# An adaLN block's modulation: rows of w_mod as TensorE weights for all columns, in place of summed and turned rows

## Chip, core and metric

The kernel runs on one core of one Trainium2 chip. Its time is the device time of one execution in microseconds (us); lower is better. The core has five engines that run their own instruction streams: TensorE (PE: matmuls, with weight loads shown apart as PEld), VectorE (DVE), ScalarE (ACT), GpSimd (POOL) and SyncE (SP, which issues nearly all DMAs).

## The reference, cut to what matters

`x` is 2048 tokens of 576, in float32. A condition vector `c` of 576 gives six vectors of 576: shift, scale and gate of an attention block (a) and of a feed-forward block (b).

```python
mod = (_silu(c) @ w_mod).reshape(c.shape[0], 6, 1, -1)
sa, ca, ga, sb, cb, gb = (mod[:, 0], ..., mod[:, 5])
h = _layernorm(x, axis=-1) * (1 + ca) + sa
x = x + ga * _A_ref(h, A_wqkv, A_wo)      # linear attention, 32 heads of 18
h = _layernorm(x, axis=-1) * (1 + cb) + sb
x = x + gb * _B_ref(h, B_w1, B_w2)        # feed-forward, 576 -> 4608 -> 576, silu
```

Nothing of the attention can be computed before `sa` and `ca` are there: the first 1152 columns of `silu(c) @ w_mod`. The change is in how these two vectors are made.

## The kernel before, in words

**Layout.** The tokens are 16 tiles of 128, in four blocks of 512. The 576 features are five chunks (`START`): four of 128 and a tail of 64. For a matmul the normalised `x` is turned so that features lie on partitions; there shift and scale of a chunk are two columns, `cols["a"][:, k, 0:2]`, each with one number per partition. `modulate` (L210) applies them, and `split_h` (L218) cuts the float32 result into a rounded part (a cast on ACT, L220) and a remainder (a subtraction on DVE, L136). Weights are cut in the same way by `w_hi` (ACT, L359) and `w_lo` (L364, L366; on DVE or POOL). Each product takes three passes: high by high, low by high, high by low.

**The first two vectors.** `silu(c)` lies in `sc`, chunk k in column k. w_mod's first 1152 columns come as five chunks of rows: `mods[0]` to `mods[3]` (128 rows each, seen as two times 576 columns) and `tmod` (the last 64 rows, with shift's columns on partitions 0 to 63 and scale's on 64 to 127). SP loads columns 0 to 255 of the four chunks first (`load_mod0(0, HEAD * P)`), then two chunks of the k weights, then the other columns.

For chunks 0 and 1 of the columns (`HEAD = 2`, 256 columns) DVE scales `mods[0]` by `sc`'s column in place (L413) and adds the three other chunks times theirs (L415). `mod_cols` (L417) then takes the sums and `tmod` as weights, 128 columns at a time, against a column of ones (`sel` for `tmod`): the result is a column per chunk in PSUM, `colp[k]`. `add_cols` (L427, one DVE instruction, L429) copies the columns of some chunks to `cols["a"]` and adds 1 to the scales.

For chunks 2 to 4 (320 columns) DVE sums in the same way (one L413 and three L415 of 640 elements). Then `mod_rows` (L431) uses `ones` and `sc` as weights and the sums and `tmod` as moving data, so that the result is a row; `copy_row` (L437) brings it to SBUF, and `turn_rows` (L443) turns it into columns, 128 numbers at a time.

**Around it.** `keep_busy(n)` (L468) issues n matmuls of ones that compute nothing; each is two records. `turn_tiles` (L450) turns tiles 0 and 1. `first_k(k)` (L519) is the k projection of these two tiles with chunk k of the features, high and low, against the high part of the weights; `k_lo` (L522) is the high part against the low part of the weights. A last `k_part` (L573) does chunks 1 to 3 against the low weights and the tail. Behind that stands the loop over tiles (L695): `v_proj(0)` (L645), `turn_half` (L461: tiles 2 and 3 are turned, modulated and split; this frees `x0` so that SP may load block 1, L292), `v_proj(1)`, `kv_mm(0)`, q of tiles 0 and 1 (`q_proj`, L660), `k_proj(2)`, `v_proj(2)`, `kv_mm(1)` and so on. `k_phi` and `q_proj` take exp on ACT (L374), a maximum on DVE (L379) and a sum of the two on DVE (L383). `ps2` gives PSUM in turn from two buffers, so v_proj(2) waits until q of tile 1 has left its buffer through L379. In each block DVE takes statistics of the next one (L191, L192), normalises it together with ACT and turns it in 32 by 32 blocks (`turn_block`, L299), which goes through DRAM into the layout with features on partitions.

**What sets the order.** PE's instructions run in the order of the program. For the others a table stands in the code: `FIRST` (L96) lists for each engine the numbers of its instructions from `begun` on, in program order, and `arrange` (L122) chains them in the order of the table. So an instruction that stands early in the table and waits holds all behind it on that engine. DVE's numbers that matter here, in the new program: 13 first scaled rows, 14 to 16 normalisation of tile 0, 17 and 18 the two other scaled rows of the head, 19 add_cols(0, 1), 20 modulate 0, 21 split 0, 22 add_cols(1, 2), 23 modulate 1, 24, 26, 27 scaled rows 1 to 3 of the other columns, 25 split 1, 28 `twice(sums)`, 29 w_lo of chunk 1, 30 add_cols(2, 3), 31 modulate 2, 32 add_cols(3, 5), 33 modulate 3, 34 to 36 splits 2 to 4, 37 w_lo of chunk 4, 38, 39, 47, 50, 51 w_lo of the v weights, 40 to 46 statistics of tiles 2 and 3, 49 and 52 the maximum and sum for k of tile 0, 53 to 56 k of tiles 0 and 1, 60 to 64 the five splits of `turn_half`, 65 to 77 statistics of block 1, 78 to 84 its normalisation and its four turns, 88 and 90 the maxima of q of tiles 0 and 1. In the old program the numbers from 33 on are 3 higher for the same instruction (66 and 67 are the splits of chunks 3 and 4 in `turn_half`, 81 to 87 the normalisation and turns of block 1, 91 and 93 the maxima of q). On ACT 24 is the exp for k of tile 0 and 27 to 30 the normalisation of tiles 2 and 3 (old 26 and 29 to 32).

Of the kernel before, what the change touches and what calls it, by code (L numbers as in the profile page):

```python
# [16 lines left out]
P = 128  # L17
# [5 lines left out]
def kernel(ctx: ExitStack, tc, A_x, A_wqkv, A_wo, B_x, B_w1, B_w2, c, w_mod, out):  # L23
# [32 lines left out]
    def behind(instructions):  # L56

        with ExitStack() as order:
# [36 lines left out]

    FIRST = {  # L96
        "DVE": """
            0 2 1 4-5 3 6-21 24-25 22-23 26 28 27 29-30 43-44 31-32 46 33-34 47 35-37 40 38 45 48-49 39 41-42 51 50
            53 52 55 54 56-58 61 60 62 88 63 89-90 64-65 68-69 71-72 70 73-75 77-78 76 79-80 91 66-67 81-87 93 59 92
            94-96 152 97 99-101 103-104 106-107 98 110-112 102 105 109 113-114 108 127-128 130-131 129 132-133 116  # L100
            134 136-137 135 138-139 115 117 140-141 119 142 120 143 121 144-146 118 122-123 153-154 124-125 155 126
            147-151 156-159 161 160 162-164 193-194 196-197 195 198-200 165 202-203 201 204-205 167 171 206-207 168
            208-212 172-174 166 175 169-170 176-184 190-191 185 192 213-215 186 219 216-217 223 187 218 220 224 221
            234 222 238 188-189 231-233 235-237 240-248 225 249-253 230 254-257 239 227 226 258-259 228 260 229
            261-263
        """,
        "Activation": """
            0-4 6-7 5 8-10 13 11-12 14-18 21 19-20 22-25 27 29 31 30 32 26 28 34 33 41-43 37 39 36 48 38 40 50 52 44
            46 56 45 57 47 49 58 51 53 35 59 54-55 60-62 65-67 70 73 63 68 64 77 71 78 69 79 75 72 80 76 81 74 82-83
            85 91 86 92 87 84 88-90 93-99 104 101 100 102 107 103 105 111 108 112 116 106 117 109 126-127 113-115 110  # L110
            118-125 128-130 133 138 134 140 131 139 144 132 141 149 135 145 136 150 137 142-143 146-148 151-170
        """,
        "Pool": """
            0-1 3-4 2 6-7 5 8-12 15-17 13-14 18-20
        """,
        "SP": """
            0-31 33 32 62 34-38 40-41 39 42-45 48-49 47 46 63-65 50-53 66 54 56-57 55 70-73 58-61 67-68 78-79 84-88
            90-91 89 92-95 80-82 69 74-77 83 96 99 98 100-102 97 106 103-105
        """,
    }  # L120

# [147 lines left out]
    def psT():  # L269
        t = psA.tile([P, 512], F32, name="psT")  # L270
        return t
# [135 lines left out]
    colp = {k: colps[k >= HEAD][:, 2 * k : 2 * k + 2] for k in START}  # L407

    def add_rows(k, c0, c1, first=False):

        o = sums[:, :, c0:c1]
        if first:
            V.tensor_scalar(o, mods[k][:, :, c0:c1], sc[:, k : k + 1], None, op0=ALU.mult)  # L413
        else:
            V.scalar_tensor_tensor(o, mods[k][:, :, c0:c1], sc[:, k : k + 1], o, op0=ALU.mult, op1=ALU.add)  # L415

    def mod_cols(k, m, rhs, first=False, last=False):  # L417

        if m is tmod:
            T.matmul(colp[k], m[:, k * P : (k + 1) * P], rhs, start=first, stop=last,  # L420
                     skip_group_check=True)
        else:
            for a in range(2):
                T.matmul(colp[k][:, a : a + 1], m[:, a, k * P : (k + 1) * P], rhs,
                         start=first and a == 0, stop=last, skip_group_check=True)

    def add_cols(k0, k1):  # L427
        src = colps[k0 >= HEAD][:, 2 * k0 : 2 * k1]
        V.tensor_add(cols["a"][:, k0:k1, :], src.rearrange("p (k a) -> p k a", a=2), plus1.unsqueeze(1).to_broadcast([P, k1 - k0, 2]))  # L429

    def mod_rows(a, part):  # L431

        h = slice(a * 64, a * 64 + 64)
        w, m = ((sc[h, KC : KC + 1], tmod[h, c1:D]) if part == 0 else (ones[:, 0:1], sums[:, a, c1:D]))
        T.matmul(rows[a][:, : D - c1], w, m, start=part == 0, stop=part == 1)

    def copy_row(a, copy):  # L437

        copy(row[a][:, 0:256], rows[a][:, 0:256])
        copy(row[a][:, 256:384].rearrange("p (h d) -> p h d", h=2),  # L440
             rows[a][:, 256:320].unsqueeze(1).to_broadcast([1, 2, 64]))

    def turn_rows(k0, k1):  # L443
        for k in range(k0, k1):
            for a in range(2):
                T.transpose(colp[k][:, a : a + 1], row[a][:, (k - HEAD) * P : (k - HEAD + 1) * P],
                            ident[0:1, 0:1])
        add_cols(k0, k1)

    def turn_tiles(pT, tiles, chunks):  # L450
        for i in tiles:
# [16 lines left out]
    def keep_busy(n):  # L468

        for _ in range(n):  # L470
            T.matmul(kvp[2][:, 1, P : 2 * P], ones, ones, start=True, stop=True, skip_group_check=True)
# [10 lines left out]
    if True:  # L482
# [24 lines left out]
        rows = [psT()[0:1], kvp[0][0:1].rearrange("p a b -> p (a b)")]  # L507
        row = [pa.tile([P, D], F32, name="e", bufs=2)[0:1] for _ in range(2)]
# [33 lines left out]
        for a in range(2):  # L542
# [1088 lines left out]
```

## Time and profile before

| what | value |
|---|---|
| three runs | 1142.91, 1141.45, 1143.43 us; median 1142.91 |
| profiled execution | 1142.39 us, span 1140.7 us |
| granted TensorE clock | 1.00 |
| DVE, ACT, POOL busy | 86%, 46%, 58% of the span |
| DMA | 279 MB in all, 245 GB/s in the mean |

The profile is of one execution. A row of the order of time has its start from the beginning of the span, its length, the engine, the line of the kernel (that of the helper where one records the operation), the operation, output and inputs by tile name, shapes and count; what stands in brackets is idle time of that engine in front of it and what ended it. Rows of one line that follow each other closely are merged, and the length is then that of the group. A line can stand for several uses: L136 is every subtraction of a split. `hT` is also the name of the room in which `mods` lies, `kvp` the PSUM rooms with the columns.

### The profile page before, as it was taken

The page shows a single profiled execution, that of the slowest core. Times are in us where ns is not written, and L with a number is a line of the kernel's source. Part 1 is how long each engine was busy: PE and PEld are TensorE (multiplying, and loading weights), DVE is VectorE, ACT ScalarE, POOL GpSimd, SP SyncE. Part 2 cuts the span into 40 slices and gives each one's busy share as a digit, 9 for nine tenths or more (in the row PEclk, how much of TensorE's full clock was granted, in tenths as well). Part 3 has the DMA queues.
Part 4 walks back from the last instruction along what each step waited for, and adds up shares of the span by engine and source line. Part 5 has one row for each costly group of instructions (what it writes and reads, how often), then busy time and mean ns, then how long its engine had stood idle before and what let it go on. Part 6 is the DMA issues. An engine that isn't in the chain of part 4 may idle for free.

```text
span 1140.7 us, 19537 instructions
## 1 busy us (share of the span) xinstructions
PE 1129.6 (99%) x7137; PEld 1042.4 (91%) x7137; DVE 986.1 (86%) x1557; ACT 526.9 (46%) x1078; POOL 658.0 (58%) x748
## 2 busy tenths in 40 slices
PE   8999999999999999999999999999999999999998
PEld 7899999899998899999999899999998999999998
DVE  7867766687988999999999899999999999999996
ACT  5544342446555544444445444444454444444441
POOL 3300000554624787667766776777667757776786
PEclk9999999999999999999999999999999999999999
DMA  9468981223468886976967969769779787697684
GB/s 290 100 155 170 184 85 37 66 73 115 161 235 295 325 317 249 351 273 250 363 263 276 328 256 349 270 253 352 274 258 342 261 333 290 255 346 269 250 310 156
DMA packets 103023, 279.05 MB, mean 245 GB/s; under 512 B 40652, under 2 KB 63440, under 8 KB 79888
## 3 DMA queue, kind: packets, MB, share of 16 engines
q1 hardware_dynamic: 102756, 277.50, 70.6%
q8 instruction: 57, 0.93, 0.3%
q10 hardware_dynamic: 172, 0.30, 0.1%
q14 instruction: 38, 0.31, 0.1%
HBM read 256.27 MB, written 21.51 MB: 244 GB/s over the span
## 4 chain that ended last, share of the span: by engine, by line
PE 93%; DMA 3%; DVE 2%; ACT 1%; issue 0%; SPq 0%; DVEq 0%; ACTq 0%
PE up L1362 33%; PE down L1435 31%; PE psK L244 12%; PE big L244 7%; PE small L925 2%; PE big L936 2%; PE kvp L671 2%; DMA hT<-hd 1%; PE psK L819 1%; PE big L851 1%; DMA room<-hd 1%; PE small L229 1%; PE up L1465 1%; PE down L1465 1%; DMA xt<-in_A_x_dram 1%; DMA hT<-in_w_mod_dram 1%
## 5 line engine op out<-in xcount | busy, mean ns | idle before, releaser
L1443 DVE TENSOR_TENSOR acc<-down,acc 128x576 f32<-128x576 f32 x330 | 246.0, 753 | 13.9 <-PE down L1435 4.1
L1362 PE MATMUL up<-hT,w 128*128 128x512 f32 x916 | 240.6, 391 | 0.4 <-DMA hT<-hd 0.4
L1362 PEld LDWEIGHTS up<-hT,w 128*128 128x128 f32 x916 | 164.5, 188 | 26.7 <-DMA hT<-hd 0.9
L1397 POOL TENSOR_TENSOR s<-f,f 128x256 f32<-128x256 f32 x66 | 51.9, 786 | 164.7 <-ACT f L1378 164.7
L1435 PE MATMUL down<-w,hc 128*128 128x288 f32 x792 | 120.8, 295 | 0.0
L1435 PE MATMUL down<-w,hb 128*128 128x288 f32 x792 | 120.7, 294 | 0.0
L1435 PEld LDWEIGHTS down<-w,hb 128*128 128x128 f32 x792 | 113.5, 188 | 6.2 <-DVE U L1443 0.4
L1435 PEld LDWEIGHTS down<-w,hc 128*128 128x128 f32 x792 | 113.7, 188 | 5.6
L1443 DVE TENSOR_TENSOR U<-down,U 128x576 f32<-128x576 f32 x132 | 99.4, 753 | 18.0 <-PE down L1435 15.7
L136 DVE TENSOR_TENSOR w<-v,w 128x288 fp32r<-128x288 f32 (+1 forms) x170 | 111.3, 664 | 0.1
L244 PE MATMUL psK<-w,hT 128*128 128x256 f32 (+1 forms) x638 | 102.4, 297 | 1.0 <-DVE acc L379 1.0
L1362 PE MATMUL up<-room,w 128*128 128x512 f32 x348 | 93.2, 396 | 0.6 <-DMA room<-hd 0.6
L244 PEld LDWEIGHTS psK<-w,hT 128*128 128x128 f32 x638 | 91.5, 189 | 1.5 <-DVE acc L379 1.5
L1416 POOL TENSOR_TENSOR hc<-s,hc 128x512 fp32r<-128x512 f32 x66 | 89.7, 1358 | 0.0
L1378 ACT ACTIVATE f<-f 128x512 f32<-128x512 f32 x102 | 64.4, 631 | 48.2 <-DVE f L1383 25.4
L1381 DVE TENSOR_TENSOR f<-up,p 128x512 f32<-128x512 f32 x102 | 69.7, 683 | 14.6 <-PE up L1362 10.0
L1362 PEld LDWEIGHTS up<-room,w 128*128 128x128 f32 x348 | 62.4, 188 | 11.9 <-DVE w L136 1.0
L1105 ACT CAST w<-v 128x288 fp32r<-128x288 f32 x85 | 36.6, 434 | 77.7 <-PE down L1435 54.7
L1401 POOL TENSOR_TENSOR f<-f,s 128x256 f32<-128x256 f32 x66 | 50.8, 770 | 34.3 <-DVE hb L1416 29.4
L197 POOL TENSOR_TENSOR rstd<-ve,neghalf 128x4 f32<-128x4 f32 (+3 forms) x10 | 10.0, 995 | 98.2 <-DVE ve L196 97.1
L1435 PE MATMUL down<-w,hd 128*128 128x288 f32 x396 | 63.2, 295 | 0.0
L1435 PE MATMUL down<-w,he 128*128 128x288 f32 x396 | 63.1, 295 | 0.0
(302 smaller groups left out, 2532.6 us busy)
## 6 DMA issues: line engine op xcount, KB each, us to landing
hT<-hd SPq DMA_DIRECT2D x66, 1280.0 KB, 6.2
hT<-hd SPq DMA_DIRECT2D x45, 1024.0 KB, 5.3
room<-hd SPq DMA_DIRECT2D x35, 1280.0 KB, 6.3
room<-hd SPq DMA_DIRECT2D x20, 1024.0 KB, 4.9
v<-in_B_w_dram SPq DMA_DIRECT2D x17, 576.0 KB, 7.3
v<-in_B_w_dram SPq DMA_DIRECT2D x17, 512.0 KB, 7.9
hd<-S SPq DMA_DIRECT2D x6, 1024.0 KB, 5.2
xt<-in_A_x_dram SPq DMA_DIRECT2D x16, 288.0 KB, 6.4
```

What stands on the lines that cost most here:

```text
L136: return V.tensor_sub(lo, full, f32(hi))
L244: T.matmul(ps, xpart(a), wpart(b), start=n == 0, stop=n == len(XW) - 1)
L671: T.matmul(o, vt[:, j, h, :], pkt[:, :, j * HG : j * HG + P], start=(t == 0 and h == 0 and j % 2 == 0), stop=(t == NT - 1 and h == 1), ski ...
L1105: A.copy(self.w2[n][:, 0], src)
L1362: T.matmul(ps, left, right, start=first and m == 0, stop=m == len(seq) - 1, skip_group_check=True)
L1378: A.activation(self.f[i, k], self.f[i, k], AF.Silu)
L1381: V.tensor_add(f, self.bank[bank[1]], self.p1)
L1397: G.tensor_add(self.s[:, 0:1], half(i, 0, 1), half(i, 1, 1))
L1401: G.tensor_sub(half(i, 1, 0), half(i, 1, 0), self.s[:, 1:2])
L1416: eng.tensor_sub(t[:, :, 1, :], src, f32(t[:, :, 0, :]))
L1435: T.matmul(ps[:, p, :HALF], self.a[i, n][:, u, p * P : (p + 1) * P], self.w.w2[n][:, v], start=n in (1, 5, 7, 6) and j == 0, stop=j == 2, ...
L1443: V.tensor_add(dst, ps[:, :, :HALF], dst)
```

## The change

Chunk 0 of w_mod's rows is no longer scaled by DVE: `mod_cols` takes it unscaled as weights against `sc[:, 0:1]`, and the sums begin with chunk 1 (`sums = mods[1]`). All five chunks of columns are made by `mod_cols`; `mod_rows`, `copy_row` and `turn_rows` go. Because the tail has 64 columns and a chunk of weights 128, `twice` copies the last 64 columns once more behind them: for `tmod` and `mods[0]` on POOL, for the sums on DVE. All columns lie in one PSUM room (`kvp[0]`), where before those of chunks 2 to 4 were in `kvp[2]`. `keep_busy` is left with 1 of 5 calls ahead of chunk 2 and its call with 2 in front of `first_k(2)`; `k_lo(0)` moves behind `first_k(1)` and the weights. The table `FIRST` is new for DVE, ACT, POOL and SP. The DMAs are the same; SP's table has small swaps.

```diff
     FIRST = {
         "DVE": """
-            0 2 1 4-5 3 6-21 24-25 22-23 26 28 27 29-30 43-44 31-32 46 33-34 47 35-37 40 38 45 48-49 39 41-42 51 50
-            53 52 55 54 56-58 61 60 62 88 63 89-90 64-65 68-69 71-72 70 73-75 77-78 76 79-80 91 66-67 81-87 93 59 92
-            94-96 152 97 99-101 103-104 106-107 98 110-112 102 105 109 113-114 108 127-128 130-131 129 132-133 116
...
+            0 2 1 4-5 3 6-7 9-10 8 11-12 14-15 13 16-24 26 25 27-31 40 32 34 33 41 35 43-44 37 42 45-46 36 38 48-49
+            39 52 47 50-51 53-55 58 57 59 85-87 60-62 65-66 68-69 67 70-72 74-75 73 76-77 88 78-84 63 90 64 56 89
+            91-93 149 96-98 94 100-101 103-105 107 95 108-109 99 102 106 110-111 124-125 127 113 128 126 129-131
...
         "Activation": """
-            0-4 6-7 5 8-10 13 11-12 14-18 21 19-20 22-25 27 29 31 30 32 26 28 34 33 41-43 37 39 36 48 38 40 50 52 44
...
+            0-4 6-7 5 8-11 13 12 14-16 19 17-18 20-23 25 24 27 29 28 30 26 31-32 39-41 35 37 34 36 46 38 48 50 42 44
...
         "Pool": """
-            0-1 3-4 2 6-7 5 8-12 15-17 13-14 18-20
+            0-1 3-4 2 6-7 5 8-14 17-19 15-16 20-22
...
-    sums = mods[0]
+    sums = mods[1]
...
-    colps = kvp[0][:, 1, 128:], kvp[2][:, 1, :]
-    colp = {k: colps[k >= HEAD][:, 2 * k : 2 * k + 2] for k in START}
+    colp = {k: kvp[0][:, 1, P + 2 * k : P + 2 * k + 2] for k in START}
...
-    def mod_cols(k, m, rhs, first=False, last=False):
...
+    def twice(m, copy):
+
+        copy(m[..., D:DX], m[..., KC * P : D])
+
+    def mod_cols(ks, m, rhs, last=False):
+
+        for k in ks:
+            if m is tmod:
+                T.matmul(colp[k], m[:, k * P : (k + 1) * P], rhs, start=k == 0, stop=last, skip_group_check=True)
+            else:
+                for a in range(2):
+                    T.matmul(colp[k][:, a : a + 1], m[:, a, k * P : (k + 1) * P], rhs,
+                             start=False, stop=last, skip_group_check=True)
...
-        ln.finish(0, 2, lambda: add_rows(0, 0, c1, True))
+        ln.finish(0, 2, lambda: add_rows(1, 0, c1, True))
...
+        head, others = range(HEAD), range(HEAD, KC + 1)
+        twice(tmod, G.tensor_copy)
         keep_busy(11)
-        for k in range(HEAD):
-            mod_cols(k, tmod, sel, first=k == 0)
+        mod_cols(head, tmod, sel)
+        mod_cols(head, mods[0], sc[:, 0:1])
         turn_tiles(pT, (0, 1), START)
-        for k in (1, 2, 3):
+        for k in (2, 3):
             add_rows(k, 0, c1)
...
         w_lo(wk_, 0, acc[0], G)
-        keep_busy(4)
-        mod_cols(0, sums, ones[:, 0:1], last=True)
+        mod_cols([0], sums, ones[:, 0:1], last=True)
         add_cols(0, 1)
-        keep_busy(1)
-        mod_cols(1, sums, ones[:, 0:1], last=True)
-        keep_busy(2)
+        mod_cols([1], sums, ones[:, 0:1], last=True)
+        mod_cols(others, tmod, sel)
         modulate(*args[0], V)
-        add_rows(0, c1, D, True)
         split_h(*args[0])
         add_cols(1, 2)
+        keep_busy(1)
         first_k(0)
+        twice(mods[0], G.tensor_copy)
+        mod_cols(others, mods[0], sc[:, 0:1])
         modulate(*args[1], V)
-        add_rows(1, c1, D)
+        add_rows(1, c1, D, True)
         split_h(*args[1])
         w_hi(wk_, 1, acc[1])
-        for a in range(2):
-            mod_rows(a, 0)
+        add_rows(2, c1, D)
+        add_rows(3, c1, D)
+        twice(sums, V.tensor_copy)
         first_k(1)
-        k_lo(0)
         w_hi(wk_, 2, acc[2])
         w_hi(wk_, 3, acc[3])
-        add_rows(2, c1, D)
-        add_rows(3, c1, D)
         w_lo(wk_, 2, acc[2], G)
         w_lo(wk_, 3, acc[3], G)
         w_lo(wk_, 1, acc[1], V)
-        mod_rows(0, 1)
-        mod_rows(1, 1)
-        copy_row(0, A.copy)
-        copy_row(1, V.tensor_copy)
-        keep_busy(4)
-        turn_rows(2, 3)
+        k_lo(0)
+        mod_cols([2], sums, ones[:, 0:1], last=True)
+        add_cols(2, 3)
         modulate(*args[2], V)
-        keep_busy(1)
-        turn_rows(3, 5)
+        mod_cols(range(3, KC + 1), sums, ones[:, 0:1], last=True)
+        add_cols(3, 5)
         modulate(*args[3], V)
         split_h(*args[2])
         keep_busy(2)
```

More of the change, by code (lines that the diff above doesn't have):

```diff
@@ L106 @@
+            133-134 132 135-136 112 116-118 137-143 114 119 115 120 150 121-122 151 123 144-146 152 147-148 153-156
+            158-160 190-191 193-194 192 195-197 199-200 198 201-202 162 203-209 165 157 161 164 168-171 163 172
+            166-167 173-181 187-188 182 189 210-212 216 220 213-214 221 215 231 217-219 235 183-185 228-229 186
+            232-234 230 237-248 222 249-254 227 236 255-257 223-224 258-260 225-226
         """,
         "Activation": """
-            0-4 6-7 5 8-10 13 11-12 14-18 21 19-20 22-25 27 29 31 30 32 26 28 34 33 41-43 37 39 36 48 38 40 50 52 44
@@ L112 @@
+            89-90 86 82 87-88 91-96 99-101 97 102 104 98 124-125 105 103 107 109 106 114 110 115 111-113 108 116-123
+            126-128 131 136 132 138 137 142 129 139 130 147 143 133 148 134-135 140-141 144-146 149-168
         """,
         "Pool": """
-            0-1 3-4 2 6-7 5 8-12 15-17 13-14 18-20
+            0-1 3-4 2 6-7 5 8-14 17-19 15-16 20-22
         """,
         "SP": """
-            0-31 33 32 62 34-38 40-41 39 42-45 48-49 47 46 63-65 50-53 66 54 56-57 55 70-73 58-61 67-68 78-79 84-88
@@ L118 @@
-            90-91 89 92-95 80-82 69 74-77 83 96 99 98 100-102 97 106 103-105
+            0-29 33 30 32 31 62 34-37 41 38 40 39 42-49 63-65 50-53 66 57 72 71 73 70 54 56 58 55 59-61 67-68 78
+            84-87 79 91 88 90 89 92-95 80-81 69 74-77 82-83 96 98-102 97 106 103-105
         """,
@@ L415, in add_rows @@
             V.scalar_tensor_tensor(o, mods[k][:, :, c0:c1], sc[:, k : k + 1], o, op0=ALU.mult, op1=ALU.add)
-    def mod_cols(k, m, rhs, first=False, last=False):
[L419 to L422, printed above, removed]
-            for a in range(2):
-                T.matmul(colp[k][:, a : a + 1], m[:, a, k * P : (k + 1) * P], rhs,
-                         start=first and a == 0, stop=last, skip_group_check=True)
+    def twice(m, copy):
[8 more added lines that the diff above has]
+                             start=False, stop=last, skip_group_check=True)
     def add_cols(k0, k1):
-        src = colps[k0 >= HEAD][:, 2 * k0 : 2 * k1]
+        src = kvp[0][:, 1, P + 2 * k0 : P + 2 * k1]
         V.tensor_add(cols["a"][:, k0:k1, :], src.rearrange("p (k a) -> p k a", a=2), plus1.unsqueeze(1).to_broadcast([P, k1 - k0, 2]))
[L431 to L448, printed above, removed]
     def turn_tiles(pT, tiles, chunks):
@@ L506 @@
         pT = rooms(ps2()[:, 0, :])
-        rows = [psT()[0:1], kvp[0][0:1].rearrange("p a b -> p (a b)")]
-        row = [pa.tile([P, D], F32, name="e", bufs=2)[0:1] for _ in range(2)]
+        head, others = range(HEAD), range(HEAD, KC + 1)
+        twice(tmod, G.tensor_copy)
         keep_busy(11)
-        for k in range(HEAD):
-            mod_cols(k, tmod, sel, first=k == 0)
+        mod_cols(head, tmod, sel)
+        mod_cols(head, mods[0], sc[:, 0:1])
         turn_tiles(pT, (0, 1), START)
-        for k in (1, 2, 3):
+        for k in (2, 3):
             add_rows(k, 0, c1)
```

10 lines of the change are left out of this document (1 added, 9 removed).

## The prediction, made before the changed kernel was run

> **What bounds the kernel now.** I read the page first, then what TensorE (PE) waited for over the whole span, then the order of time of the first 58 us, and last the chain of waits through that stretch.
>
> ```profile
> span 1140.7 us, 19537 instructions
> ...
> PE 1129.6 (99%) x7137; PEld 1042.4 (91%) x7137; DVE 986.1 (86%) x1557; ACT 526.9 (46%) x1078; POOL 658.0 (58%) x748
> ...
> PEclk9999999999999999999999999999999999999999
> ```
>
> PE is busy for 99% of the span, so a microsecond counts only if PE gets it; the granted clock is full in every slice. The profiled execution took 1142.39 us, 1.7 us more than its span and 0.5 us less than the median of the three runs (1142.91). In the rows on waits (what waited, for whom, total, times, longest) four places matter:
>
> ```profile
> PE psK L244 <- DVE acc L379: 1.0, 1, 1.0
> PE kvp L420 <- ACT xt L206: 1.0, 1, 1.0
> PE psT L244 <- DVE w L366: 0.7, 1, 0.7
> PE kvp L471 <- DVE col_a L429: 0.7, 2, 0.4
> ```
>
> All lie in the first 52 us. But "busy" hides more: L471 is `keep_busy`, matmuls that compute nothing. Real work runs without such fillers only from 22.29 on. So the change acts in front of 22.29, and the question is how much of it reaches the time at which v_proj(2) starts (51.53), since behind that PE is busy without a gap up to 200 us (the first and the last of four windows from 60 us on, with PE's busy time behind the comma):
>
> ```profile
> 60.00:80.00 20.00, 20.00 (x152) 20.00 (x152) 12.99 (x29) 10.15 (x18) 0.00 (x0) 1.00 0.84 214
> ...
> 140.00:200.00 60.00, 60.00 (x459) 60.00 (x458) 37.41 (x62) 21.57 (x46) 2.33 (x5) 1.00 0.47 65
> ```
>
> These are rows of the order of time (start, length, engine, line), from the first scaled rows of w_mod to the k projection of tiles 0 and 1:
>
> ```profile
> 7.55 0.49 DVE L413 TENSOR_SCALAR hT<-hT,sc 128x512 f32<-128x512 f32 x1 [1.74 <-DMA hT<-in_w_mod_dram]
> ...
> 8.03 0.92 DVE L208 TENSOR_SCALAR xt<-xt,mv,rstd 128x64 f32<-128x64 f32 x2
> ...
> 8.86 2.32 DVE L415 SCALAR_TENSOR_TENSOR hT<-hT,sc 128x512 f32<-128x512 f32 x3
> ...
> 11.24 0.61 PE L424 MATMUL kvp<-ones,hT 128*128 128x1 f32 x4
> 11.38 1.40 POOL L364 TENSOR_TENSOR v<-acc,w 128x576 fp32r<-128x576 f32 x1 [4.75 <-ACT w L359]
> ...
> 11.88 0.16 DVE L429 TENSOR_TENSOR col_a<-kvp,plus 128x2 f32<-128x2 f32 x1 [0.70 <-PE kvp L424]
> 12.08 0.54 DVE L216 TENSOR_SCALAR raw<-psK,col_a 128x256 f32<-128x256 f32 x1
> ...
> 12.66 0.41 ACT L220 CAST hT<-raw 128x256 fp32r<-128x256 f32 x1 [0.59 <-DVE raw L216]
> ...
> 13.40 0.54 DVE L413 TENSOR_SCALAR hT<-hT,sc 128x640 f32<-128x640 f32 x1
> ...
> 13.86 0.41 DVE L136 TENSOR_TENSOR hT<-raw,hT 128x256 fp32r<-128x256 f32 x1
> ...
> 14.19 1.80 DVE L415 SCALAR_TENSOR_TENSOR hT<-hT,sc 128x640 f32<-128x640 f32 x2
> ...
> 16.24 0.88 DVE L415 SCALAR_TENSOR_TENSOR hT<-hT,sc 128x640 f32<-128x640 f32 x1
> ...
> 16.50 1.89 POOL L364 TENSOR_TENSOR w<-acc,w 128x576 fp32r<-128x576 f32 x1 [3.72 <-DMA acc<-in_A_wqkv_dram]
> ...
> 17.04 1.97 DVE L364 TENSOR_TENSOR w<-acc,w 128x576 fp32r<-128x576 f32 x1
> ...
> 17.63 0.70 PE L435 MATMUL psT<-hT,ones 128*1 128x320 f32 x2
> ...
> 18.36 1.92 POOL L364 TENSOR_TENSOR w<-acc,v 128x576 fp32r<-128x576 f32 x1
> ...
> 18.93 0.81 DVE L191 BATCH_NORM_STATS2 st<-xt 128x6 f32<-128x288 f32 x2
> ...
> 20.55 0.13 DVE L429 TENSOR_TENSOR col_a<-kvp,plus 128x2 f32<-128x2 f32 x1
> ...
> 22.29 1.31 PE L477 MATMUL psK<-w,hT 128*128 128x288 f32 x8
> ```
>
> Read it backwards. The k projection of chunk 2 (22.29) waits for the column of the modulation (`add_cols(2, 3)`, 20.55), that one for rows turned on PE, copied (L439, L440) and summed (L435, 17.63), and those for the fourth scaled row on VectorE (DVE), ended at 17.12. DVE is full from 12.9 to 22; it, not PE, sets this stretch.
>
> **The change part by part.** (1) *The head.* One of three L415 (2.32 / 3 = 0.77) goes from the first 256 columns, and the first L413 now scales row 1 in place of row 0. But the new table puts it (13) between the two normalisations of tile 0 (15, 16), and row 1's data came later than row 0's. It had come by 8.86, where L415 used it without a wait; I take 8.8 (the other end is 7.5, when row 0 came). Then L413 0.49, the large normalisation 0.58 (of the 0.92), two L415 1.55, less overlaps: the sums are there at about 11.3 against 11.18. Nothing is gained; the other end is 0.8 gained. PE's eight added passes for row 0 (0.61 / 4 = 0.15 each, 1.1 us between 9.0 and 10.1) fit in the place of `keep_busy(4)`, eight records of nothing, which goes.
>
> (2) *Columns 2 to 4.* Removed: one scaled row (0.9), the row matmuls, four copies, six transposes. Added: nine matmuls with tmod and row 0 as weights and six with the sums (two records of up to 0.15 each), two small copies on POOL and one on DVE. POOL is idle from 12.78 to 16.50; PE needs its copy of row 0's tail at about 14.6, and even at the 1.40 of L364 it would be there at 14.2. DVE's queue from 12.0, in the new table's order (16-24 26 25 27-31), is: add_cols 0.16, modulate 0.54, wait for the cast on ACT 0.41, split 0.41, add_cols 0.16, modulate 0.54, L413 0.54, L415 0.90, split 0.41, L415 0.90: with overlaps, about 16.7. In the old order it hid the cast's wait behind chunk 1, so leaving a row out gives only 0.4 here. Behind it stand `twice(sums)` and `w_lo` of chunk 1 (29), and only then `add_cols(2, 3)` (30). PE meets it early enough: first_k(0), twelve records of row 0, first_k(1), k_lo(0) and four records end at about 18.1.
>
> The two ops in between decide. `w_lo` took 1.97 at 17.04, beside POOL's L364 at 16.50 and 18.36; with POOL idle it takes 0.75:
>
> ```profile
> 24.56 0.75 DVE L364 TENSOR_TENSOR v<-acc,w 128x576 fp32r<-128x576 f32 x1
> ```
>
> POOL's two ops start when their weights land (16.50), which the change doesn't move, so I take 1.97 again (the other end is 0.75, below as a rival). The trace has no copy of this shape in this place; the nearest is
>
> ```profile
> 199.84 0.20 DVE L782 COPY tmod<-tmod 128x64 f32<-128x64 f32 x1
> ```
>
> With twice the elements that is about 0.25, and stretched like `w_lo` (1.97 / 0.75) about 0.7. I take the middle, 0.5, since it runs beside POOL, but L415 at 16.24 was not stretched there. So `add_cols(2, 3)` comes at 16.7 + 0.5 + 1.97 = 19.1 (18.9 to 19.4) against 20.55: 1.4 us earlier. [...]
>
> (3) *To the end of v_proj(0).* Of four L191 of tiles 2 and 3, three had been done in the old wait (18.93 on); now all follow `add_cols(2, 3)`: some 1.2 us more for DVE before chunk 4's split. The new table gives most of it back further down: ACT's exp of kps[0] (24) now precedes the four normalisations, and with it DVE's idle 1.56 goes.
>
> ```profile
> 28.94 0.76 DVE L379 TENSOR_SCALAR a<-psK 128x576 f32<-128x576 f32 x1 [1.56 <-ACT e L374]
> ...
> 31.34 0.38 PE L244 MATMUL psT<-w,hT 128*128 128x256 f32 x1 [0.68 <-DVE w L366]
> ```
>
> From 19.1 DVE has two modulates (0.54), three splits (0.41, two of them behind casts of 0.41), four L191 (0.41), the half w_lo (0.76), add_cols behind PE's eight records (0.9), and 0.45 of small ops: the split of chunk 4 ends at 24.6. Then w_lo, max, w_lo, min, three w_lo, at 0.7 each with a wait of 0.5 for the exp: the last w_lo ends at about 30.1. PE's last passes of v_proj(0) start there rather than at 31.34: **1.2 us earlier** (0.95 to 1.45), of the 1.4.
>
> (4) *The next block.* The transposes of tiles 2 and 3 follow, and they free the room for the load of block 1. This is the order of time there:
>
> ```profile
> 33.32 3.17 SPq L292 DMA_DIRECT2D xt<-in_A_x_dram  x4
> ...
> 45.87 1.01 POOL L197 TENSOR_TENSOR rstd<-ve,neghalf 128x4 f32<-128x4 f32 x1 [6.02 <-DVE ve L196]
> 46.36 0.75 DVE L136 TENSOR_TENSOR hT<-raw,hT 128x256 fp32r<-128x256 f32 x2
> ...
> 48.08 2.75 DVE L299 STREAM_TRANSPOSE acc<-xt 128x576 f32<-128x576 f32 x4
> ...
> 50.76 0.72 DVE L379 TENSOR_SCALAR acc<-psK 128x576 f32<-128x576 f32 x1
> ...
> 51.53 0.54 PE L244 MATMUL psK<-w,hT 128*128 128x256 f32 x2 [1.05 <-DVE acc L379]
> ```
>
> All of it hangs on the load and moves with it, 1.2 us to the front. But the two L136 at 46.36, the splits of chunks 3 and 4 for tiles 2 and 3, ran while DVE waited for POOL's rstd (to 46.88) and cost nothing. In the old table they are 66-67, ahead of 81-87; in the new one 63 and 64 come behind 78-84, with 90 between. So, counted from the end of L299 (50.83 in the old): split 0.38, max of q tile 1 0.69, split 0.35, then PE's last pass of k_proj(2), 0.06 + 0.27: v_proj(2) starts 1.75 behind L299, where it was 0.70. k_proj(2) stands still in its twelfth pass for it. **1.05 us is given back.**
>
> (5) *The rest.* The other moves in the tables behind 52 us I cost at nothing: PE has no wait from 52 to 200 in the old, and the entries moved (94, 105, 157, 161, 164, 168) still stand ahead of their readers by 0.2 us or more in my count. Without that cover each could cost some 0.5.
>
> Sum: 1.2 - 1.05 = 0.15, say 0.2 us gained: 1142.39 - 0.2 = **1142.2** (against the median of before 0.7 less, of which 0.5 is that execution's own distance).
>
> **The rivals.** *The start's gain is kept*: if block 1's load comes late or PE late enough that the two splits hide again, (4) costs nothing: 1142.39 - 1.2 = 1141.2. The old wait of 1.05 in front of 51.53 shows that DVE is last there, so I doubt it.
>
> *No stretch on DVE, and kept*: w_lo at 0.75 and the copy at 0.25 would bring `add_cols` to PE's own 18.2: 2.3 us gained, 2.1 of it at v_proj(0), 1140.3. Against it stands the row at 17.04.
>
> *It does not do what it says*: with the first sums late (data of row 1 at 9.5 rather than 8.8) and a stretched copy, columns 2 come no earlier than before; (4) remains: 1143.4.
>
> *Slower, by the array's rate*: in the old, `keep_busy(4)`, `(1)` and `(2)` stood between the rows and chunk 2, of 14 records at two a matmul; four remain, and PE stands idle for some 1 us before 19.1 and again around first_k(3) and chunk 4. At the start of the kernel the same dummies ran at half the later rate, which the granted clock of the page doesn't show:
>
> ```profile
> 1.12 3.73 PE L471 MATMUL kvp<-ones 128*128 128x128 f32 x16 [1.12 <-DVE sel L485]
> ...
> 4.94 2.72 PE L471 MATMUL kvp<-ones 128*128 128x128 f32 x22
> ```
>
> That is 0.23 against 0.12 each. If such pauses bring the slow rate back, the 36 real passes up to v_proj(0) take 4.3 us more, less 1.8 in which they wait anyway, and v_proj(0) runs slow for another 3.7, losing 1.9: 4.4 us, 1146.6. It decides if PE's pauses are long enough; the 1.0 us in front of L420 slowed nothing behind it (0.15 a record). [...]
>
> **How the numbers follow.** Forecast 0.52, gain kept 0.17, no stretch and kept 0.07, does nothing 0.12, slow array 0.12. The likeliest case is 1142.2. About 0.2% (2.3 us) is what a measurement of this kernel can tell from no change, around 1142.9: faster is the case without stretch and the edge of the kept gain, 0.10; slower the slow array and an unseen stall of the new tables, 0.15; the rest, 0.75, is no change. The range holds all but the slow array: from 1140.3 (no stretch, kept) to 1144.4 (does nothing, and two stalls of 0.5 us behind 52 us).
>
> **What would show it.** Right: `add_cols` of two columns (L429) near 19.1, `w_lo` beside POOL at about 2 us, the load L292 near 32.1, and a wait of PE of about 1 us inside k_proj(2), put down to L136, with v_proj(2) near 51.3. Wrong: L429 later than 20; no PE wait on L136 near 49; PE records at 0.2 us and more behind 19; new PE waits behind 52 us.

## The result, and the profile after

The changed kernel takes **1146.07 us** (median of 7 runs, 1145.41 to 1148.79) against 1143.36 (7 runs, 1141.45 to 1144.46) for the kernel before: ratio 1.0037 [1.0026, 1.0047] (the brackets hold the 95% interval), slower by 0.4%. The prediction was 1142.2, from 1140.3 to 1144.4. The profiled execution of the changed kernel took 1148.79 us, 6.4 more than that of before (1142.39).

From the page of the changed kernel: its span, its engines, and the granted clock in 40 slices of 28.7 us.

```profile
span 1147.1 us, 19539 instructions
...
PE 1135.6 (99%) x7139; PEld 1051.5 (92%) x7139; DVE 985.0 (86%) x1554; ACT 525.8 (46%) x1076; POOL 657.9 (57%) x750
...
PEclk6999999999999999999999999999999999999999
```

PE is 6 us longer "busy" (1135.6 against 1129.6), and the first digit of the clock, a 9 before, is a 6. Windows over that slice (from and to, length, PE's busy time with its records, granted clock, share and rate of the DMAs) show where:

```profile
5.00:10.00 5.00, 3.81 (x33) 1.00 1.09 308
10.00:15.00 5.00, 4.75 (x28) 0.61 1.07 371
15.00:20.00 5.00, 5.00 (x23) 0.50 1.05 304
20.00:25.00 5.00, 4.75 (x22) 0.50 1.05 304
25.00:30.00 5.00, 5.00 (x23) 0.50 0.70 214
30.00:40.00 10.00, 9.75 (x68) 0.92 0.01 3
```

And windows of 0.2 us give both edges:

```profile
10.86:11.06 0.20, 0.20 (x5) 0.99 1.03 365
11.06:11.26 0.20, 0.20 (x4) 0.50 1.06 371
31.34:31.54 0.20, 0.20 (x2) 0.51 0.00 0
31.54:31.74 0.20, 0.20 (x3) 1.00 0.00 0
```

TensorE ran at half rate from 11.06 to 31.54 us: 20.48 us. Cut in the same way, the traces of the experiments below have half rate for 3.41 us (e3, twice in e9, and once in e8 between 25 and 30 us), 6.83 (e1, e4), 10.24 (e8, e12) and 13.65 (e14): whole numbers of 3.41, here six (e3's is in its window from 20 to 25 us below: 0.66 in the mean is 3.4 us at half rate). Such a piece of 3.41 us is called a stretch from here on. In every slice of 10 to 30 us PE counts as busy for 95% and more of the time. What ran in front of the fall, from the order of time on PE:

```profile
8.79 0.58 PE L422 MATMUL kvp<-sel,tmod 128*128 128x2 f32 x4 [1.19 <-DMA tmod<-in_w_mod_dram]
9.23 1.03 PE L425 MATMUL kvp<-sc,hT 128*128 128x1 f32 x8
10.12 0.41 PE L435 MATMUL psK<-ident,xt 128*128 128x128 f32 x2
```

A pause of 1.19, twelve records one or two columns wide, and then turns. In the old kernel the turns began at 9.13 and eight wide dummies followed from 10.26. What the half rate cost, in rows of the order of time:

```profile
17.47 2.55 PE L425 MATMUL kvp<-sc,hT 128*128 128x1 f32 x12
...
19.89 2.27 PE L459 MATMUL psK<-w,hT 128*128 128x288 f32 x8
...
20.66 0.23 DVE L416 COPY hT<-hT 128x128 f32<-128x128 f32 x1
...
20.80 0.75 DVE L363 TENSOR_TENSOR w<-acc,w 128x576 fp32r<-128x576 f32 x1
...
23.80 0.16 DVE L430 TENSOR_TENSOR col_a<-kvp,plus 128x2 f32<-128x2 f32 x1 [2.24 <-PE kvp L425]
...
37.50 0.39 PE L243 MATMUL psT<-w,hT 128*128 128x256 f32 x1 [0.25 <-DVE w L365]
...
39.47 2.51 SPq L291 DMA_DIRECT2D xt<-in_A_x_dram  x4
```

Eight k passes take 2.27 (1.31 in the old kernel at 22.29). `add_cols(2,3)` comes at 23.80, not at the 19.1 forecast, and DVE now waits 2.24 for PE there. v_proj(0) gets its last passes at 37.50 (31.34), block 1's load goes out at 39.47 (33.32), and v_proj(2) starts at 58.02 (51.53): 6.5 us, the whole difference. From there to the end both profiled executions take the same, 1089.0 and, before, 1089.1.

The seven runs also differ among themselves in step with the clock: 1148.79 and 1148.38 at a mean granted clock of 0.991, 1147.09 at 0.992, 1146.07 and 1145.86 at 0.993, 1145.41 at 0.995 and 1145.69 at 0.996. One stretch at half rate takes 0.0015 off that mean (1.7 of 1145 us), so these are about six to three stretches, and about 1 us is lost with each.

### The profile page after: what moved, and what is told of

It is laid out like the page before. It is cut to its first block, busy times and chain, and to the rows that moved or that the text cites. A ratio compares the mean times of both kernels' runs of the same rounds, so it can differ in the third digit from the quotient of the medians.

```text
span 1147.1 us, 19539 instructions
## 1 busy us (share of the span) xinstructions
PE 1135.6 (99%) x7139; PEld 1051.5 (92%) x7139; DVE 985.0 (86%) x1554; ACT 525.8 (46%) x1076; POOL 657.9 (57%) x750
## 4 chain that ended last, share of the span: by engine, by line
PE 95%; DMA 2%; DVE 1%; ACT 1%; issue 0%; SPq 0%; ACTq 0%; POOL 0%; DVEq 0%
PE up L1340 33%; PE down L1413 32%; PE psK L243 12%; PE big L243 7%; PE small L903 2%; PE big L914 2%; PE kvp L649 2%; PE psK L459 1%; PE psK L797 1%; PE big L829 1%; DMA hT<-hd 1%; DMA room<-hd 1%; PE kvp L425 1%; PE small L228 1%; PE up L1443 1%; PE down L1443 1%
```

## The experiments

**Theory A**: the loss is the half rate. The change took away wide matmuls and put one-column passes on PE in their place, and the clock follows the amount of wide work in a stretch of about 3.4 us. **Theory B**: the added passes and VectorE's new queue cost the time by themselves. **Theory C**: the pause of 1.19 (1.03 before) brings the clock down by its length. Line numbers are those of the changed kernel, one to some twenty lower than in the old one. The number of stretches in a run is worked out as (1 - mean granted clock) x span / 1.71; the mean is over the whole span, so it does not say where they lie. The kernel before ran beside each group of experiments on the same chip: 1142.39 (35 runs) beside e1 to e4, 1142.37 (31) beside e5 to e8, 1142.19 (27) beside e9 to e11, 1142.33 (21) beside e12 to e14. Times are medians, ratios are to before.

**e1: wide dummies in the pause only.**

```diff
-        keep_busy(11)
+        keep_busy(15)
```

> The changed kernel with keep_busy(15) for keep_busy(11): eight more 128x128 matmuls in TensorE's idle 7.6 to 8.8 us, where it waits for the first tmod columns; nothing else. Theory A (the granted clock falls for want of wide matmul work in the stretch of some 3.4 us that ends at 11.06; that costs about 1.1 us for each 3.41 us at half rate): full clock past 11.06; as the later dummies are still missing, half rate may come later, so 1142 to 1145, granted clock at least 0.995. Theory B (the added column passes and VectorE's new queue cost the time, the clock is a side effect): within 0.5 us of the changed kernel, about 1146. Theory C (the length of the pause alone, 1.19 us against 1.03, drops the clock): full clock throughout, 1142 to 1143.

1145.66 us, ratio 1.0030 [1.0013, 1.0047], two to seven stretches in the 12 runs. The pause is gone (its rest was 0.5 on the tmod data), and the loss stays: **theory C fails.** In the profiled run the clock held at 11 us and fell at 14.31. The time is 0.7 above theory A's range and within theory B's, so this run alone does not part these two.

**e2: the old four dummies back in their place.**

```diff
+        keep_busy(4)
         mod_cols([0], sums, ones[:, 0:1], last=True)
```

> The changed kernel with keep_busy(4) put back in its old place, ahead of chunk 0's passes with the sums; nothing else. There it begins at about 11.2 us, behind the point at which the clock fell (11.06). Theory A (amount of wide work in the stretch up to 11.06): the clock still falls at 11.06, but wide work in the next stretches is more, so half rate lasts shorter: 7 to 14 us, 1144 to 1146. Theory B (passes and VectorE's queue): 0 to 0.5 us later than the changed kernel, 1146 to 1146.6. Theory C (pause): falls at 11.06 as before, for the same length, 1146.

1146.14, ratio 1.0021 [1.0006, 1.0036], one to five stretches. By the time alone the three theories can't be told apart here (A had 1144 to 1146, B and C 1146 and a little more). In the profiled run the half rate was shorter than the 20.48 us above, as A said: 10.82 to 14.23 and 17.65 to 24.47, three stretches. One place alone does not do it.

**e3: dummies in all the gaps.**

```diff
-        keep_busy(11)
+        keep_busy(15)
...
+        keep_busy(2)
         mod_cols([0], sums, ones[:, 0:1], last=True)
         add_cols(0, 1)
+        keep_busy(1)
         mod_cols([1], sums, ones[:, 0:1], last=True)
...
-        keep_busy(1)
+        keep_busy(2)
         first_k(0)
...
         k_lo(0)
+        keep_busy(2)
         mod_cols([2], sums, ones[:, 0:1], last=True)
...
+        keep_busy(1)
         mod_cols(range(3, KC + 1), sums, ones[:, 0:1], last=True)
```

> The changed kernel with dummies enough in all gaps: keep_busy(15) for (11), and (2), (1), (2), (2), (1) ahead of the passes with the sums for chunk 0, 1, the first k passes, chunk 2 and chunks 3 and 4. Theory A: granted clock 1.0 in every 5 us window, add_cols(2,3) near 19.1, block 1's load near 32.1, and 1142.2 (1141.7 to 1143.0), which is what the prediction gave for the change without the half rate. Theory B: the clock is full, but the time stays at 1145 to 1147. Theory C: as A.

**1141.63**, ratio 0.9989 [0.9976, 1.0001]; 9 of 12 runs at full clock, median of these 1141.52. The added passes and the queue are all still there, with 22 records more on PE, and the kernel is 4 us faster than e1 and e2 on the same chip: **theory B fails.** The expected full clock in every window was not quite had; the profiled run lost one stretch behind 21 us:

```profile
10.00:15.00 5.00, 4.87 (x41) 1.00 1.07 371
15.00:20.00 5.00, 4.42 (x37) 1.00 1.05 328
20.00:25.00 5.00, 4.89 (x27) 0.66 1.05 328
```

**e8: the same dummies, one column wide.** As e3, with

```diff
-    def keep_busy(n):
+    def keep_busy(n, w=P):
...
-            T.matmul(kvp[2][:, 1, P : 2 * P], ones, ones, start=True, stop=True, skip_group_check=True)
+            T.matmul(kvp[2][:, 1, P : P + w], ones, ones[:, 0:w], start=True, stop=True, skip_group_check=True)
```

and `w=1` for the dummies that e3 adds (`keep_busy(4, 1)` behind the old `keep_busy(11)`, and so on).

> As e3, but all the dummies added to the changed kernel read and write one column in place of 128: as many records on TensorE, about as long in the trace, at the same places. If the width of a matmul counts for the clock: the clock falls as in the changed kernel (mean 0.992 to 0.996), time 1145 to 1147. If being busy is enough: as e3, mean clock 0.999 and 1141.6 to 1142.3.

1147.03, ratio 1.0031 [1.0015, 1.0046], three to six stretches. Its windows:

```profile
5.00:10.00 5.00, 5.00 (x41) 1.00 1.07 316
10.00:15.00 5.00, 4.97 (x37) 0.79 1.07 371
15.00:20.00 5.00, 5.00 (x24) 0.50 1.06 289
20.00:25.00 5.00, 4.97 (x30) 0.68 1.05 292
25.00:30.00 5.00, 5.00 (x28) 0.66 0.72 221
```

PE is busy for 4.97 of 5 us and more in each, with hardly a pause, more than in e3, and the clock falls all the same. e3 and e8 have the same records in the same places, with the same waits; only the width differs. (They ran on two chips, on which before took 1142.39 and 1142.37.) Here the same records kept PE busy and lost the clock in all 8 runs when they were narrow, and kept it in 9 of 12 when they were wide.

**e4 and e9: dummies taken from the old kernel.** e4 takes out `keep_busy(4)` ahead of chunk 0's passes. e9 leaves it only the dummies of the changed kernel:

```diff
-        keep_busy(4)
         mod_cols(0, sums, ones[:, 0:1], last=True)
...
-        keep_busy(1)
         mod_cols(1, sums, ones[:, 0:1], last=True)
-        keep_busy(2)
+        keep_busy(1)
...
-        keep_busy(4)
         turn_rows(2, 3)
...
-        keep_busy(1)
         turn_rows(3, 5)
```

> The kernel before without keep_busy(4) ahead of chunk 0's passes with the sums (10.26 to 11.32 us); nothing else, so neither columns nor queues are changed, and the pause ahead of the tmod columns stays at 1.03 us. Theory A: the clock falls to half near 11 us and the kernel gets 1 to 5 us slower, 1144 to 1148. Theory B: the clock may fall, the time stays within 0.5 us of before (1143.4). Theory C: the clock stays full, time as before.

> The kernel before, with its rows, turns and queues untouched, but only the dummies that the changed kernel has: (4), (1), (4), (1) go and (2) ahead of the first k passes becomes (1). Theory A (the loss is the dummies' going, through the clock): three to six stretches of 3.41 us at half rate, mean clock 0.991 to 0.996, 1145 to 1148, as the changed kernel. Theory B (the added passes and the new queue): within 0.5 us of before.

Both fell short of theory A's numbers: e4 1143.43, ratio 0.9999 [0.9987, 1.0012]; e9 1143.20, ratio 1.0004 [0.9995, 1.0013]. The clock did fall (e9: one to three stretches in every run), but not for long, and 1 us of median is all that went, which the ratios don't tell from nothing. So the dummies' going is not the whole cause. What had been left out of theory A is what stands in their place in the changed kernel. e12 and e13 test that, each from its own side.

**e12: e9 with narrow records added.** At the places of the changed kernel's added passes, in their numbers (a `keep_busy(1, 1)` is two records one column wide):

```diff
+        keep_busy(4, 1)
         turn_tiles(pT, (0, 1), START)
...
         mod_cols(1, sums, ones[:, 0:1], last=True)
+        keep_busy(3, 1)
         keep_busy(1)
...
         first_k(0)
+        keep_busy(6, 1)
```

> e9 (the old kernel with only the dummies of the changed one) and one-column dummies in the numbers and at the places at which the changed kernel has its added one-column passes: 8 records ahead of the turns, 6 ahead of the first k passes, 12 behind them. If the narrow passes make the half rate last (theory A, completed): three to six stretches, mean clock 0.992 to 0.996, and 1144.5 to 1147. If the new order of the waits does (theory D): as e9, two to three stretches, and 1143.2, at most 0.5 more for the records' own time.

**1147.81** (5 runs, 1146.47 to 1151.18), ratio 1.0041 [1.0027, 1.0056]: the old order of waits, tables and engines, and a loss like that of the changed kernel, even 1.9 larger (e14 below). One window of e9 and one of e12, of the same 5 us:

```profile
15.00:20.00 5.00, 4.96 (x25) 0.85 1.05 318
```

```profile
15.00:20.00 5.00, 5.00 (x24) 0.50 1.06 323
```

This loss is not the clock's alone. In the profiled runs the start has two stretches in e9 and three in e12, yet v_proj(2) starts at 52.32 and 56.26: the 26 added records also take PE's own time, 5.6 us in e12's trace (1.03, 2.05 and 2.55, most of it at half rate). And the slowest run of e12, which is the profiled one, has two more stretches at 381 us, behind a wait of PE of 2.8 for a DMA. So e12 (three to five stretches a run, e9 one to three) shows that narrow records bring the clock down in the old order too; what the clock costs is better read from pairs with equal numbers of records, e3 and e8, e13 and e14.

**e13: the changed kernel with wide records in place of its added passes**, and no dummy restored:

```diff
-        mod_cols(head, mods[0], sc[:, 0:1])
+        wide(4)
...
-        mod_cols(others, tmod, sel)
+        wide(3)
...
-        mod_cols(others, mods[0], sc[:, 0:1])
+        wide(6)
```

where `wide` is the matmul of `keep_busy`. The shares of the modulation that these passes compute are left out, and with them PE's waits for their data.

> The changed kernel, no dummies restored, but its added column passes (row 0 for all columns, 20 records, and tmod for columns 2 to 4, 6 records) are replaced by as many 128x128 matmuls of ones into the dummies' room. This leaves row 0's share and, for columns 2 to 4, the share of the last rows out of the modulation. If the passes' width decides: the clock is full or nearly so (mean 0.998 to 1.0) and the time 1141.5 to 1143 without one dummy more. If the new order of the waits decides: half rate for three stretches and more, 1145 to 1146.

**1141.49**, ratio 0.9990 [0.9979, 1.0002], 9 of 11 runs at full clock (the two others 1142.02 and 1146.81; in the profiled one, the first of these, the lost stretch is at 50.5 us):

```profile
10.00:15.00 5.00, 4.18 (x33) 1.00 1.07 371
15.00:20.00 5.00, 4.65 (x40) 1.00 1.05 331
20.00:25.00 5.00, 4.75 (x34) 1.00 1.06 321
```

Beside it on the same chip **e14**, the changed kernel unaltered:

> The changed kernel unaltered, for a comparison on the same chip: mean clock 0.991 to 0.996 by execution, median 1145 to 1146, and about 1 us more for each stretch at half rate, so that the times fall towards 1141.5 at full clock.

1145.93, ratio 1.0033 [1.0022, 1.0044], three to six stretches; medians 1144.5 at three, 1145.5 at four, 1147.4 at five, 1148.5 at six. e13 has fewer busy microseconds from 10 to 25 us than the changed kernel (13.6 against 14.5) and full clock. e13 alone would leave open whether the dropped waits did it; e3 and e8 have the same waits and differ as much. With both pairs the cause is shown: the width of PE's records in this part of the kernel.

How much wide work is enough can be estimated from the traces. Cut the time from the first full clock (at 4 to 7 us) to 47 us into stretches of 3.41 us by each trace's own edges, and add up in each the moving columns of PE's matmul records (128 for a record of a wide dummy, 1 for one of a narrow dummy). In the 16 traces, eleven of the twelve stretches right ahead of a fall have 70 to 1883 columns (the twelfth, in e8, 2452); of the 164 at full clock with full clock behind them, three have fewer than 1900 (1578, 1805, 1839). PE's busy share does not part them: it goes up to 0.99 ahead of a fall and down to 0.75 where the clock held. This is a count, not a limit that a run tried, and two later falls had more columns and long pauses: 2800, busy 0.53 (e13 at 50.5 us), and 2713, busy 0.38 (e12 at 381 us).

**e5: the two splits ahead of the turns again**, on top of e3, in VectorE's table:

```diff
-... 73 76-77 88 78-84 63 90 64 56 89
+... 73 76-77 88 63-64 78-84 90 56 89
```

> The kernel with dummies in all gaps (e3) and one more edit: in VectorE's table the splits of chunks 3 and 4 for tiles 2 and 3 (63 and 64) stand ahead of the turns of block 1 (78-84) again, as in the old table. The prediction's step 4 says that they cost about 1.05 us behind the turns; in the trace of e3 PE waited there 0.71 and 0.20 us. If that is right: the wait of PE on hT L135 near 50 us goes, v_proj(2) starts 0.7 to 1.0 us earlier counted from the load of block 1, and the kernel is 0.5 to 1.0 us faster than e3: 1140.6 to 1141.2 on the chip where before takes 1142.4 (ratio to before near 0.998). Rival: what PE gains there it loses at a later wait behind 52 us: time as e3, ratio near 0.9990.

1141.27, ratio 0.9989 [0.9979, 0.9999]; its 8 runs at full clock have 1140.68, and four lost two stretches (1142.45). The median is therefore little below e3's, but at full clock e5 stands 1.7 below the runs of before at full clock on its chip (1142.35), and e3 0.6 below those on its own (1142.12): 1.1 between them. The traces tell it without the clock. e3:

```profile
47.27 2.75 DVE L298 STREAM_TRANSPOSE acc<-xt 128x576 f32<-128x576 f32 x4
...
50.39 0.53 PE L243 MATMUL psK<-v,hT 128*128 128x288 f32 x2 [0.71 <-DVE hT L135]
...
51.39 0.80 PE L243 MATMUL psK<-w,hT 128*128 128x288 f32 x4 [0.20 <-DVE hT L135]
```

e5:

```profile
46.87 2.75 DVE L298 STREAM_TRANSPOSE acc<-xt 128x576 f32<-128x576 f32 x4
...
50.32 0.54 PE L243 MATMUL psK<-w,hT 128*128 128x256 f32 x2 [0.31 <-DVE acc L378]
```

From the turns to v_proj(2) it is 3.45 in before and in e5, 4.49 in e3 and 4.48 in the changed kernel: 1.04 more. So it is in all traces: 3.44 or 3.45 in the nine with the splits ahead of the turns, 4.48 to 4.54 in the seven with them behind.

**e6 and e7: w_lo of chunk 1 behind the columns.** e6 adds to e5, in the same table,

```diff
-... 16-24 26 25 27-31 40 32 34 33 41 35
+... 16-24 26 25 27-28 30-31 40 32 34 33 29 41 35
```

and e7 also moves the `keep_busy(2)` ahead of chunk 2's passes behind them.

> As e5, and w_lo of chunk 1 on VectorE (29 in the table) goes from ahead of add_cols(2,3) to behind add_cols(3,5) and the split of chunk 2, when POOL's w_lo is nearly done. The prediction's rival without stretch: add_cols(2,3) goes from 19.9 (e3) to about 18.9, where PE's passes with the sums end, the w_lo takes 0.75 in place of 1.97, and v_proj(0)'s last passes come 1 to 2 us earlier: ratio to before 0.9970 to 0.9978. Rival: VectorE's other work behind it (normalisation, splits, five w_lo of v) sets the end of v_proj(0) whatever the column does: ratio as e5.

> As e6, with the two dummies ahead of chunk 2's passes with the sums moved behind them (three ahead of chunks 3 and 4, where PE waits for add_cols(2,3) anyway). If PE sets add_cols(2,3) in e6, the column comes 0.4 us earlier still and the time is 0 to 0.4 us below e6; if VectorE's copy of the sums (to 18.1) sets it, the same as e6.

e6: **1140.60**, ratio 0.9978 [0.9969, 0.9987], full clock in all 12 runs. With e10 (below) it is the version most clearly faster than both kernels, by 1.8 us against before. But w_lo's move did little of it:

```profile
17.11 1.36 DVE L416 COPY hT<-hT 128x128 f32<-128x128 f32 x1
...
19.49 0.16 DVE L430 TENSOR_TENSOR col_a<-kvp,plus 128x2 f32<-128x2 f32 x1 [1.02 <-PE kvp L425]
...
21.66 0.75 DVE L363 TENSOR_TENSOR w<-acc,w 128x576 fp32r<-128x576 f32 x1
```

w_lo fell to 0.75 as expected, and the column came 0.7 earlier than in e5 (19.49, 20.16), yet the last passes of v_proj(0) only 0.2 (31.04, 31.23), and at full clock e6 and e5 have the same time (1140.61, 1140.68). That fits the rival of that run, by which VectorE's work behind the column sets the end of v_proj(0). e7 took 1142.26, ratio 0.9993 [0.9981, 1.0005]: 1140.66 in its 6 runs at full clock, but 6 of 12 lost one stretch or more. Why e6 kept the clock in all runs and e5 in two thirds is not settled by 12 runs each.

**e10 and e11: the pause alone.** e10 is e6 with `keep_busy(11)` again, e11 the old kernel with `keep_busy(15)`.

> As e6, but keep_busy(11) in place of (15) ahead of the tmod columns, so that the pause of 1.0 to 1.2 us there is open again; all later dummies stay. If the wide work in the stretch around the pause and the narrow passes decides (theory A): the clock falls near 11 us in most executions, in the others not, by where the stretches of 3.41 us lie; mean clock 0.996 to 0.999, median 1141 to 1144. If only the work behind 11 us matters: clock 1.0 and 1140.6, as e6.

> The kernel before with keep_busy(15) for (11), nothing else: its own pause of 1.03 us is filled. In 12 of 35 and 6 of 31 of its runs the clock was below full. By theory A these go: mean clock 1.0 in all runs, median 1142.1 to 1142.4, highest below 1144; that is then the fair base for e6 (1140.6). By chance of another kind: as many runs below full as before.

Both came out against what theory A gave. e10: 1140.13, ratio 0.9984 [0.9975, 0.9993], 9 of 11 at full clock with the pause open. e11: 1142.52, ratio 0.9999 [0.9990, 1.0008], 4 of 11 runs below full clock with the pause filled (before, beside it: 4 of 27). No effect of the pause is to be seen.

## Why the prediction was wrong, point by point

- **The step that failed** is in (1): PE's eight passes for row 0 "fit in the place of `keep_busy(4)`, eight records of nothing, which goes". They fit in time, which is all that the step weighed; for the clock, dummies out and narrow passes in were put at nothing, and so were the further narrow passes of (2). The runs show half rate instead: 20.48 us of it in the profiled execution, with v_proj(2) at 58.02 where about 51.3 was forecast. The size of the term is 4.4 us in medians (e14 less e13), and 4.0 to 4.5 by e1 and e2 against e3. The dummies' going alone costs about 1 (e4, e9); it is the narrow passes in their place that make it last.
- **The rival "by the array's rate"** named the effect, and the prediction listed its sign, PE records of 0.2 us and more behind 19 (eight passes took 2.27, 0.28 each). It got 0.12 because its condition was wrong: "It decides if PE's pauses are long enough" looked at idle time. The clock fell at 11.06 with one pause of 1.19 in the 3.4 us ahead, and in e8 with next to none (5.00 and 4.97 us busy in the 5 us on either side of 10 us). The row held against the rival, the 1.0 us pause that slowed nothing, was a row in which wide turns and eight dummies followed at once. That its price (1146.6) came near the median (1146.07) is in part luck: it charged a fixed run of passes, where the executions lost three to six stretches and took 1145.41 to 1148.79.
- **The head**, (1): the sums were to be there at 11.3; PE took them at 11.37 in e3. Right.
- **Columns 2 to 4**, (2): in e3, whose clock was full up to there, `add_cols(2,3)` came at 19.91, against 19.1. Every term stood but one, the copy of the sums, in the rows beside POOL:

```profile
16.52 1.49 POOL L363 TENSOR_TENSOR w<-acc,w 128x576 fp32r<-128x576 f32 x1 [3.60 <-ACT w L358]
...
16.75 1.34 DVE L416 COPY hT<-hT 128x128 f32<-128x128 f32 x1
...
17.97 1.40 POOL L363 TENSOR_TENSOR w<-acc,v 128x576 fp32r<-128x576 f32 x1
...
18.01 1.97 DVE L363 TENSOR_TENSOR w<-acc,w 128x576 fp32r<-128x576 f32 x1
...
19.91 0.15 DVE L430 TENSOR_TENSOR col_a<-kvp,plus 128x2 f32<-128x2 f32 x1
```

  `w_lo` took the 1.97 forecast; the copy took 1.34 where 0.5 was taken and 0.7 was the upper end, scaled from `w_lo`'s own stretch. In the changed kernel itself, with POOL done, the copy took 0.23 and w_lo 0.75 (20.66, 20.80): the other end of both ranges. Beside POOL the copy was thus stretched nearly six times, `w_lo` 2.6 times. The scaled row that the prediction held against a stretch (0.88 at 16.24) had begun ahead of POOL's op at 16.50; in the changed kernel the one at 18.60, beside POOL's at 18.36, took 2.02.
- **v_proj(0) and the load**, (3): 1.2 earlier was forecast (load near 32.1). e5, at full clock and with the changed kernel's order up to there, had it at 33.20, 0.1 earlier than before; with the copy's 0.84 off, 0.4 was due. Single profiles don't settle tenths here: the old kernel with its pause filled (e11), at full clock, had the load at 34.68, 1.4 later than before.
- **The next block**, (4): 1.05 given back was forecast, 1.04 measured, and 1.03 to 1.1 between any two traces that differ in it. From the load to the turns e3 and e5 took 13.6 where before took 14.8, which made up for (3); but that is no gain of the change, since the old order took from 13.64 (e9) to 14.99 (e11) there and the new one from 13.41 (e8) to 14.53 (e2). What sets it was not tried.
- **The rest**, (5): put at nothing. From v_proj(2) to the end before took 1089.1 and the changed kernel 1089.0; the other traces took 1087.9 to 1089.6, old and new order alike, but for e12 (1093.2, with the wait of 2.8 for a DMA). No loss there is to be seen, within that scatter.
- **The sum** at full clock: 0.2 us gained was forecast; e3 has 0.6 to 0.8 by medians and 1.3 by its ratio, with an interval that reaches 0. That the sum came near is in part luck: (4) and (5) held, (3) fell short, and the scatter of single executions is larger than what it gave. The term that decided was not in it.

## What to carry to other kernels

Before taking out or replacing a filler, ask what it fills: on PE a record of 128 columns and a record of one column last about as long in the trace (in e3 30 of the first took 3.62 us, 8 of the second 1.03), but where the same added records had 128 columns the clock was full in 9 of 12 runs (e3), and where they had one, in none of 8 (e8). Count the columns that the passes move in each 3.4 us of a start or a sparse part, not the busy share (an estimate from the count over the 16 traces: some 1900, fifteen records of 128, as the least for this kernel; the limit was not measured), and price the loss as half rate for several such stretches (three to six in the changed kernel, about 1 us each). Read the mean granted clock of every run beside its time: when times scatter in step with it, compare at equal clock first, and only then ask what the edit did.

## What the runs showed of the hardware that was not expected

- In e8, with the added dummies one column wide, the granted clock fell to 0.50 while PE showed 99 to 100% busy; with the same records 128 wide (e3) it was full in 9 of 12 runs. In the changed kernel it stayed at 0.50 for six stretches of 3.41 us and came back at 31.54, behind passes of 288 columns from 26.59 on.
- The edges lie elsewhere from one execution to the next: the fall was at 11.06 in the changed kernel's profile and at 14.18 in that of e14, the same code. The number of lost stretches of that code runs from three to six (e14).
- A copy of 128x128 on VectorE took 0.23 with POOL idle (20.66 in the changed kernel) and 1.34 beside POOL's subtraction (16.75 in e3), nearly six times as long; `w_lo` 0.75 (20.80 in the changed kernel) and 1.97 (18.01 in e3); in the changed kernel a scaled row of 640 columns 0.88 (16.25, begun ahead of POOL's op at 16.84) and 2.02 (18.60, beside the next).
